# Dense layers in token blocks of 512 with a last one of 256, gated product written over the gates, weight steps a block sooner

## The chip, the cores and the metric

One core of a Trainium2 chip runs the whole kernel in one launch. The metric is device time in microseconds, from the start of the launch to its end. TensorE (PE) multiplies, VectorE (DVE), ScalarE (ACT) and GpSimd (POOL) work on elements, SyncE (SP) issues most DMAs. Each engine takes its instructions strictly in the order in which the kernel emits them, and waits on semaphores of the others.

## The reference: what is computed

Attention with a threshold, then a layer that mixes tokens and has a wide hidden layer, then a gated layer with a causal convolution. Four batches of 576 tokens, 512 channels, 2304 tokens in all:

```python
# attention: 4 batches, 8 heads, 576 tokens, 64 channels each -> x (4, 576, 512)
h = xt @ U @ V                                  # rank 32, over tokens
u = x + h.transpose(0, 2, 1)
ch = np.maximum(u @ w_ch1, 0.0) @ w_ch2         # 512 -> 2048 -> 512
x = u + ch
...
gate_pre += conv_w[k] * xp[:, k:k + S, :]       # 5 taps, causal
gate = 1.0 / (1.0 + np.exp(-gate_pre))
val = x @ w_val
return gate * val @ w_out
```

The change concerns the part from `u @ w_ch1` on.

## The kernel before

**Operands in two halves.** The dense layers multiply in a rounded float format. To keep accuracy each operand is held as a high half (rounded) and a low half (the rest), and each product is three matmuls: high x high, high x low, low x high. `passes` (line 732) does this for one output tile of 128 channels: 4 pieces of 128 input channels by three, 12 matmuls into one PSUM bank. The weights are the stationary side (128 x 128), the tokens the moving one.

**Token blocks.** Tokens lie along the free dimension. All 2304 are cut into NN blocks of NB = 384 (lines 70 and 71), six of them, whatever the batch bounds; `runs(n)` (line 709) gives the pieces of a block by batch.

**Chunks.** The hidden layer of 2048 is done in four chunks of 512 (`items`: chunk c outside, block n inside). For each (c, n), `h1` (line 740) makes the hidden block: 4 x 12 matmuls into the tiles named `a`, per tile a ReLU on ScalarE into the high half of `h` and the low half on VectorE. `ch` (line 789) multiplies it by the second weight, 4 x 12 matmuls into tiles named `c`, and VectorE adds them into `y`. `back` of an item is emitted one item later, so that TensorE does h1 of block n+1 before ch of block n. `split_block` (line 718) makes the two halves of the next block's input `us` (ScalarE, then VectorE); `us` has one buffer, so it is written after the h1 that reads the last one and before the next, while TensorE does a ch.

**The front.** The first two h1 are emitted piece by piece among the last steps of attention (`dense_front`, line 752), to fill TensorE there; `mix_t` and `mix_u` (lines 521 and 531) and the copies of lines 439, 481, 540 and 547 are attention's own.

**Weights.** They come as 64 bit floats. `weight_rows` (line 153) is a generator: a DMA, then about ten steps on ScalarE, VectorE and GpSimd (lines 99 to 127, 162, 164) that turn 128 x 512 of them into two halves. `chunk(c, part)` (line 698) puts four such generators into `work`; each `tick` advances those that live (four at most) by one step. So where weight operations stand among the others follows from where `chunk` is called and how often `tick` is. w1 and w2 have two buffers each, by turns for even and odd chunks.

**Gates.** When all of a batch's y is there (last chunk), `gate_step` (line 807) goes on with its gates, one step per call: ScalarE makes the first tap, VectorE four more (line 819), ScalarE the sigmoid. The gates are written over `u`. `tick` calls it once, or twice in proj.

**val and proj.** `val(n)` (line 852) multiplies y by w_val into tiles `v`; VectorE multiplies by the gate into one of two buffers of `ring` (line 863), ScalarE rounds that to the high half of `g`, VectorE makes the low half. `proj(n)` (line 871) multiplies by w_out, 128 tokens at a time with 512 output channels as moving columns (line 879), ScalarE copies into `ring`, and SyncE sends 256 KB out. The order at the end: val(0), the last ch, val(1), proj(0), val(2), proj(1), and so on.

Of the kernel before, what the change touches and what calls it, by code (L numbers as in the profile page):

```python
# [21 lines left out]
F32 = mybir.dt.float32  # L22
# [14 lines left out]
def attention_moe_kernel(  # L37
# [29 lines left out]
    TL = S - SM  # L67
    HS = S // 2
    T = B * S
    NB = 384  # L70
    NN = T // NB
    YP = S + KC - 1
    assert D == 64 and S == 576 and DM == 512 and R == 32 and TL == 64

# [8 lines left out]
    qscale = const.tile([128, 1], F32, name="qscale")  # L83
    cw = const.tile([128, KC, KD], F32, name="cw")
    u = const.tile([128, KD, T], F32, name="u")
    ring = const.tile([128, 2560], F32, name="ring")
    w1_0 = const.tile([128, 2, KD, FC], F32R, name="w1_0")
    w2_0 = const.tile([128, 2, KD, FC], F32R, name="w2_0")
    wst_p = ctx.enter_context(tc.tile_pool(name="wst", bufs=2))
# [60 lines left out]
        return w[0:m, 0:n]  # L150


    def weight_rows(dst, kk, src, lo_eng, *opt):
# [11 lines left out]
        done.append(0)  # L165


    class Staged:
# [524 lines left out]


    p1 = {}
    w1, w2 = [[w1_0], []], [[w2_0], []]

    def chunk(c, part):
        if c < NCH:
            src = w_ch2[c * FC:(c + 1) * FC, :] if part else w_ch1[:, 2 * c * FC:2 * (c + 1) * FC]  # L700
        else:
            src = w_out if part else w_val
        for kk in range(KD):
            work.add(weight_rows((w2 if part else w1)[c % 2], kk, src[kk * 128:(kk + 1) * 128, :],
              nc.vector if c == 0 and part else nc.gpsimd,
              *((0, 1) if c == 0 and not part else ())))


    def runs(n):
        got, done = [], 0  # L710
        while done < NB:
            b, s = divmod(n * NB + done, S)
            m = min(NB - done, S - s)
            got.append((done, m, b, s))
            done += m
        return got
# [10 lines left out]
        return t  # L727

    def u_src(n):
        return [(0, NB, u[:, :, n * NB:(n + 1) * NB])]  # L730

    def passes(ps, w, x, e):
        ops = []
        for kk in range(KD):
            wh, wl = w[:, 0, kk, e * 128:(e + 1) * 128], w[:, 1, kk, e * 128:(e + 1) * 128]
            ops += [(wh, x[:, 0, kk, :]), (wh, x[:, 1, kk, :]), (wl, x[:, 0, kk, :])]
# [3 lines left out]
    def h1(c, us):  # L740
        t = p1["h"].tile([128, 2, KD, NB], F32R, tag="h", name="h")
        for e in range(KD):
            ps = p1["a"].tile([128, 512], F32, tag="a", name="a")
            passes(ps, w1[c % 2][0], us, e)
            nc.scalar.activation(out=t[:, 0, e, :], in_=ps[:, 0:NB], func=ACTF.Relu)  # L745
            nc.vector.scalar_tensor_tensor(  # L746
                out=t[:, 1, e, :], in0=ps[:, 0:NB], scalar=0.0, in1=f(t[:, 0, e, :]), op0=ALU.max, op1=ALU.subtract
            )
            yield t


    def dense_front():
        p1["us"] = ctx.enter_context(tc.tile_pool(name="us", bufs=1, side="right"))
        p1["h"] = ctx.enter_context(tc.tile_pool(name="h", bufs=2, side="right"))
        p1["a"] = ctx.enter_context(tc.tile_pool(name="a_ps", bufs=4, space=PSUM))
        p1["t"] = []
        us = split_block(u_src(0), p1["us"])
        yield
        while len(done) < 1 + KD:
            yield  # L760
        us2 = None
        for t in h1(0, us):
# [4 lines left out]
        for t in h1(0, us2):  # L767
            yield
        p1["t"].append(t)
        yield  # L770
        p1["s"] = split_block(u_src(2), p1["us"])
# [4 lines left out]
    def dense_back():  # L776
        extra.close()
        low.close()
        big = ctx.enter_context(tc.tile_pool(name="big", bufs=1))
        p1["y"] = big.tile([128, KD, B, YP], F32, name="y")  # L780
        w1[1].append(big.tile([128, 2, KD, FC], F32R, name="w1_1"))
        w2[1].append(big.tile([128, 2, KD, FC], F32R, name="w2_1"))
        nc.gpsimd.memset(p1["y"][:, :, :, 0:KC - 1], 0.0)

    def dense():
        y = p1["y"]
        c_ps = ctx.enter_context(tc.tile_pool(name="c_ps", bufs=4, space=PSUM, side="right"))

        def ch(c, n, t):
            for e in range(KD):  # L790
                ps = c_ps.tile([128, 512], F32, tag="c", name="c")
                passes(ps, w2[c % 2][0], t, e)
# [34 lines left out]

        def tick(n=1):
            work.tick()
            for _ in range(n):  # L830
                gate_step()

# [17 lines left out]
        turn = {"g": 0, "o": 0}  # L850
# [19 lines left out]

        def proj(n, t):
            w = w2[NCH % 2][0]
            for g in range(NB // 128):
# [25 lines left out]
        work.finish()  # L899
        work.add(setup_cw())  # L900
        for idx, (c, n) in enumerate(items):
            if idx >= 2:
                for t in h1(c, us):
                    tick()
                held.append((c, n, t))
                us = split_block(u_src(items[idx + 1][1]) if idx + 1 < len(items) else y_src(0))
            if n == 1:
                chunk(c + 1, 0)
                chunk(c + 1, 1)
            if idx:  # L910
                back(*held.pop(0))
        pt = None
        for n in range(NN):
            t = val(n, us)
# [42 lines left out]
```

## Time and profile before

| | |
|---|---|
| timed runs | 880.66 us median of three, 878.94 to 881.77 |
| profiled execution | 882.26 us, its span 880.5 us |
| mean granted TensorE clock | 0.982 |
| TensorE busy | 837.9 us (95%) |
| VectorE busy | 616.9 us (70%) |
| ScalarE, GpSimd busy | 443.7 us, 212.7 us |
| bytes moved | 69.76 MB |

The page of the profile cuts the span into 40 slices of 22 us and gives each engine's busy share in tenths. In a timeline or a chain of waits each row has a start and a length in us, then the engine, the line of the kernel and how many instructions are merged; the length runs to the end of the last one. Matmuls are pipelined, so a run of them is priced by the starts of what stands before and behind, or by the chain, which gives the time until the next link. A bracket at the end names idle time ahead of the row and who ended it. Records of one engine overlap by a little under 0.1 us.

### The profile page before, as it was taken

The page shows a single profiled execution, that of the slowest core. Times are in us where ns is not written, and L with a number is a line of the kernel's source. Part 1 is how long each engine was busy: PE and PEld are TensorE (multiplying, and loading weights), DVE is VectorE, ACT ScalarE, POOL GpSimd, SP SyncE. Part 2 cuts the span into 40 slices and gives each one's busy share as a digit, 9 for nine tenths or more (in the row PEclk, how much of TensorE's full clock was granted, in tenths as well). Part 3 has the DMA queues.
Part 4 walks back from the last instruction along what each step waited for, and adds up shares of the span by engine and source line. Part 5 has one row for each costly group of instructions (what it writes and reads, how often), then busy time and mean ns, then how long its engine had stood idle before and what let it go on. Part 6 is the DMA issues. An engine that isn't in the chain of part 4 may idle for free. (4 is left out here: it accounts for less than half of the span.)

```text
span 880.5 us, 15063 instructions
## 1 busy us (share of the span) xinstructions
PE 837.9 (95%) x5480; PEld 773.9 (88%) x5480; DVE 616.9 (70%) x1368; ACT 443.7 (50%) x916; POOL 212.7 (24%) x304
## 2 busy tenths in 40 slices
PE   6868999999999999999999999999999999999998
PEld 5756878787878788889999999999999999998896
DVE  2775988989898988435664576546774489988850
ACT  2556887878888878522332333222331244435532
POOL 1323443433332322003242033202221023400000
PEclk7798999999999999999999999999999999999999
DMA  5764766675755544001121021101120012000111
GB/s 127 159 140 97 167 153 142 149 165 130 178 127 122 123 105 110 1 1 48 48 73 48 1 79 66 49 1 48 48 72 25 1 52 69 25 1 36 62 47 72
DMA packets 71076, 69.76 MB, mean 79 GB/s; under 512 B 49621, under 2 KB 54357, under 8 KB 71002
## 3 DMA queue, kind: packets, MB, share of 16 engines
q1 hardware_dynamic: 70058, 68.50, 31.8%
q8 instruction: 44, 0.72, 0.3%
q10 hardware_dynamic: 944, 0.30, 0.2%
q14 instruction: 30, 0.25, 0.1%
HBM read 35.44 MB, written 4.72 MB: 46 GB/s over the span
## 5 line engine op out<-in xcount | busy, mean ns | idle before, releaser
L738 PE MATMUL c<-h,w 128*128 128x384 f32 x1152 | 206.9, 338 | 1.2 <-ACT u L547 1.2
L738 PE MATMUL a<-us,w 128*128 128x384 f32 x1152 | 207.5, 338 | 0.0
L738 PEld LDWEIGHTS c<-h,w 128*128 128x128 f32 x1152 | 202.9, 188 | 1.5 <-ACT u L547 1.5
L738 PEld LDWEIGHTS a<-us,w 128*128 128x128 f32 x1152 | 202.7, 188 | 0.4 <-issue 0.4
L745 ACT ACTIVATE h<-a 128x384 fp32r<-128x384 f32 x96 | 47.0, 490 | 177.6 <-PE a L738 177.6
L127 POOL TENSOR_TENSOR wf<-wf,wt 128x512 f32<-128x512 f32 (+2 forms) x42 | 60.0, 1429 | 284.6 <-DVE wt L122 281.0
L403 POOL TENSOR_TENSOR th<-nm,tau_eff 128x1 f32<-128x1 f32 x144 | 74.6, 519 | 221.6 <-DVE ns L388 220.9
L413 DVE SCALAR_TENSOR_TENSOR e<-ns,th,e 128x576 f32<-128x576 f32 x144 | 121.0, 840 | 9.6 <-ACT e L402 8.6
L388 DVE TENSOR_SCALAR_CACHE_REDUCE ns<-s 128x576 f32<-128x576 f32 x144 | 107.7, 748 | 26.6 <-PE s L374 25.9
L746 DVE SCALAR_TENSOR_TENSOR h<-a,h 128x384 fp32r<-128x384 f32 x96 | 53.4, 556 | 104.1 <-ACT h L745 104.1
L402 ACT ACTIVATE e<-ns,nm 128x576 f32<-128x576 f32 x144 | 111.4, 773 | 28.5 <-DVE ns L388 26.1
L374 PE MATMUL s<-st 128*128 128x288 f32 x504 | 100.3, 321 | 2.3 <-DMA st<-qk 1.3
L430 PE MATMUL xm<-idn,e 128*128 128x128 f32 x576 | 88.3, 276 | 2.9 <-DVE qk L299 1.1
L439 ACT ACTIVATE pt<-xm 128x512 f32<-128x512 f32 x144 | 84.6, 587 | 6.3 <-PE xm L430 3.4
L374 PEld LDWEIGHTS s<-st 128*128 128x128 f32 x504 | 72.7, 192 | 15.0 <-issue 5.6
L430 PEld LDWEIGHTS xm<-idn,e 128*128 128x128 f32 x576 | 70.2, 142 | 6.4 <-ACT pt L439 2.3
L484 PE MATMUL o<-pt,vt 128*64 128x256 f32 (+1 forms) x768 | 71.6, 337 | 0.0
L484 PEld LDWEIGHTS o<-pt,vt 128*64 128x64 f32 x768 | 42.4, 141 | 25.5 <-issue 11.7
L796 DVE TENSOR_TENSOR y<-c,y 128x384 f32<-128x384 f32 (+1 forms) x96 | 40.5, 447 | 32.1 <-PE c L738 32.1
L162 ACT ACTIVATE w<-wf 128x512 fp32r<-128x512 f32 x40 | 25.2, 629 | 72.6 <-POOL wf L127 72.6
L819 DVE SCALAR_TENSOR_TENSOR u<-y,cw,u 128x576 f32<-128x576 f32 x64 | 58.5, 920 | 0.4
L723 DVE TENSOR_TENSOR us<-u,us 128x768 fp32r<-128x768 f32 x48 | 53.6, 1156 | 5.9 <-ACT us L722 5.9
(99 smaller groups left out, 1038.4 us busy)
## 6 DMA issues: line engine op xcount, KB each, us to landing
raw<-in_moe_w_ch_dram SPq DMA_DIRECT2D x32, 512.0 KB, 3.9
st<-qk SPq DMA_DIRECT2D x32, 256.0 KB, 4.1
st<-qk SPq DMA_DIRECT2D x16, 432.0 KB, 4.0
st<-qk SPq DMA_DIRECT2D x48, 144.0 KB, 4.3
st<-qk SPq DMA_DIRECT2D x16, 288.0 KB, 4.9
out_dram<-ring SPq DMA_DIRECT2D x18, 256.0 KB, 2.0
qn<-in_q_dram SPq DMA_DIRECT2D x32, 128.0 KB, 3.5
kn<-in_k_dram SPq DMA_DIRECT2D x32, 128.0 KB, 4.0
```

Source lines behind the costliest of these rows:

```text
L127: nc.gpsimd.tensor_tensor(out=dst, in0=dst, in1=tf, op=ALU.add)
L374: nc.tensor.matmul(s[:, n, 0:HS], lhs, rhs[:, n * HS:(n + 1) * HS], start=(m == 0), stop=(m == len(ops) - 1))
L388: nc.vector.tensor_scalar(out=ns.rearrange("p (a b) -> p a b", a=2), in0=s, scalar1=-1.0, scalar2=3.0e38, op0=ALU.mult, op1=ALU.min, accum ...
L402: nc.scalar.activation(out=row(p, i), in_=d["ns", i], func=ACTF.Exp, bias=nm[:, 0:1], scale=-1.0)
L403: nc.gpsimd.tensor_tensor(out=th, in0=nm, in1=tau_eff, op=ALU.add)
L413: nc.vector.scalar_tensor_tensor(out=e, in0=d.pop(("ns", i)), scalar=d.pop(("th", i))[:, 0:1], in1=e, op0=ALU.is_le, op1=ALU.mult, accum_o ...
L430: nc.tensor.transpose(x[:, j * 128:(j + 1) * 128], e[:, c + j * 128:c + (j + 1) * 128], idn)
L439: later(s + 1, 0, lambda: nc.scalar.activation(out=dst, in_=x.rearrange("p (j c) -> p j c", j=4), func=ACTF.Copy), "x")
L484: nc.tensor.matmul(o, lhs, rhs, start=False, stop=stop)
L723: nc.vector.tensor_tensor(out=t[:, 1, e:e + 2, o:o + m], in0=s[:, e:e + 2], in1=f(t[:, 0, e:e + 2, o:o + m]), op=ALU.subtract,)
L738: nc.tensor.matmul(ps[:, 0:NB], lhs, rhs, start=(m == 0), stop=(m == len(ops) - 1))
L819: nc.vector.scalar_tensor_tensor(out=g, in0=y[:, e, b, k:k + S], scalar=cw[:, k, e:e + 1], in1=g, op0=ALU.mult, op1=ALU.add)
```

## The change

NB becomes 512, so that there are four blocks of 512 tokens and a last one of 256; all operations take the block's own size. Other parts of the change:

- The gated product is written over the gates in `u`, not into `ring`, which is cut to what proj and the set-up need.
- w2's second buffer moves to a pool of its own on the other side of SBUF.
- `chunk(c + 1)` is called when n = 0, behind `back`, not when n = 1, ahead of it. Every second tick advances the weight steps twice. `need` makes sure that the steps of a weight are emitted before the matmuls that read it.
- ch calls `tick(2)`: two gate steps per tile.

```diff
-    NB = 384
-    NN = T // NB
+    NB = 512
+    NN = -(-T // NB)
+    size = [min(NB, T - n * NB) for n in range(NN)]
...
-    ring = const.tile([128, 2560], F32, name="ring")
+    ring = const.tile([128, 1280 + S // 2], F32, name="ring")
...
+    def need(c, part):
+        while len(rows[c, part]) < KD:
+            work.tick()
...
-            nc.tensor.matmul(ps[:, 0:NB], lhs, rhs, start=(m == 0), stop=(m == len(ops) - 1))
+            nc.tensor.matmul(ps[:, 0:m1], lhs, rhs, start=(m == 0), stop=(m == len(ops) - 1))
...
-        w2[1].append(big.tile([128, 2, KD, FC], F32R, name="w2_1"))
+        w2_p = ctx.enter_context(tc.tile_pool(name="w2", bufs=1, side="right"))
+        w2[1].append(w2_p.tile([128, 2, KD, FC], F32R, name="w2_1"))
...
         def ch(c, n, t):
+            need(c, 1)
...
-                tick()
+                tick(2)
...
         def tick(n=1):
             work.tick()
+            turn["w"] ^= 1
+            if turn["w"]:
+                work.tick()
...
-                passes(ps, w1[NCH % 2][0], ys, e)
-                o = 2 * DM + turn["g"] % 2 * NB
-                g = ring[:, o:o + NB]
-                turn["g"] += 1
-                nc.vector.tensor_tensor(out=g, in0=ps[:, 0:NB], in1=u[:, e, n * NB:(n + 1) * NB], op=ALU.mult)
-                nc.scalar.activation(out=t[:, 0, e, :], in_=g, func=ACTF.Copy)
-                nc.vector.tensor_tensor(out=t[:, 1, e, :], in0=g, in1=f(t[:, 0, e, :]), op=ALU.subtract)
+                m = size[n]
+                passes(ps, w1[NCH % 2][0], ys, e, m)
+                g = u[:, e, n * NB:n * NB + m]
+                nc.vector.tensor_tensor(out=g, in0=ps[:, 0:m], in1=g, op=ALU.mult)
+                nc.scalar.activation(out=t[:, 0, e, 0:m], in_=g, func=ACTF.Copy)
+                nc.vector.tensor_tensor(out=t[:, 1, e, 0:m], in0=g, in1=f(t[:, 0, e, 0:m]), op=ALU.subtract)
...
         for idx, (c, n) in enumerate(items):
+            need(c, 0)
             if idx >= 2:
-                for t in h1(c, us):
+                for t in h1(c, us, n):
                     tick()
                 held.append((c, n, t))
                 us = split_block(u_src(items[idx + 1][1]) if idx + 1 < len(items) else y_src(0))
-            if n == 1:
+            if idx:
+                back(*held.pop(0))
+            if n == 0:
                 chunk(c + 1, 0)
                 chunk(c + 1, 1)
-            if idx:
-                back(*held.pop(0))
+        need(NCH, 0)
+        need(NCH, 1)
```

What this moves on TensorE is shown by the end of the program. Before, from the last h1 (`a`) over the last two ch (`c`) to the first proj (`p`); `v` is val:

```order
L738 MATMUL a<-us,w_1_5525 128x384 x48
L738 MATMUL c<-h,w_1_5526 128x384 x48
L738 MATMUL v<-us,w_0_66 128x384 x48
L738 MATMUL c<-h,w_1_5526 128x384 x48
L738 MATMUL v<-us,w_0_66 128x384 x48
L879 MATMUL p<-w_0_67,g 128x512 x36
```

And now the same stretch:

```order
L745 MATMUL a<-us,w_1_5525 128x256 x48
L745 MATMUL c<-h,w_1_5529 128x512 x48
L745 MATMUL v<-us,w_0_66 128x512 x48
L745 MATMUL c<-h,w_1_5529 128x256 x48
L745 MATMUL v<-us,w_0_66 128x512 x48
L891 MATMUL p<-w_0_67,g 128x512 x48
```

The sequence is the same; what stands between the two val blocks is now the narrow ch.

VectorE, before, from the split for the first val block (`us<-y`) to the first val product: `u<-y,cw,u` is a gate step, `y<-c,y` the sum of ch, `wt` a weight operation.

```order
L723 TENSOR_TENSOR us<-y,us 128x768 x2
L796 TENSOR_TENSOR y<-c,y 128x192 x2
L122 SCALAR_TENSOR_TENSOR wt<-raw,wt 128x512
L819 SCALAR_TENSOR_TENSOR u<-y,cw,u 128x576
L796 TENSOR_TENSOR y<-c,y 128x192 x2
L819 SCALAR_TENSOR_TENSOR u<-y,cw,u 128x576
L796 TENSOR_TENSOR y<-c,y 128x192 x2
L819 SCALAR_TENSOR_TENSOR u<-y,cw,u 128x576
L796 TENSOR_TENSOR y<-c,y 128x192 x2
L819 SCALAR_TENSOR_TENSOR u<-y,cw,u 128x576
L863 TENSOR_TENSOR ring<-v,u 128x384
```

VectorE now, from the c block of n = 2 in the last chunk, where the last weight operations stand:

```order
L806 TENSOR_TENSOR y<-c,y 128x128
L806 TENSOR_TENSOR y<-c,y 128x384
L113 TENSOR_SCALAR wt<-wf 128x512
L109 SCALAR_TENSOR_TENSOR wf<-raw,wt 128x512
L123 SCALAR_TENSOR_TENSOR wt<-raw,wt 128x512
L113 TENSOR_SCALAR wt<-wf 128x512
L829 SCALAR_TENSOR_TENSOR u<-y,cw,u 128x576 x2
L806 TENSOR_TENSOR y<-c,y 128x128
L806 TENSOR_TENSOR y<-c,y 128x384
L123 SCALAR_TENSOR_TENSOR wt<-raw,wt 128x512
L829 SCALAR_TENSOR_TENSOR u<-y,cw,u 128x576 x2
```

The last weight operation has moved from the ch ahead of the first val block to the ch before that one, and gate steps stand two by two.

## Rows read from the trace of the kernel before

**Rows 1.** The page: TensorE's busy time, its 40 slices, the granted clock.

```profile
PE 837.9 (95%) x5480; PEld 773.9 (88%) x5480; DVE 616.9 (70%) x1368; ACT 443.7 (50%) x916; POOL 212.7 (24%) x304
...
PE   6868999999999999999999999999999999999998
...
PEclk7798999999999999999999999999999999999999
```

**Rows 2.** Waits of TensorE from 355 us on: us in total, times, longest.

```profile
PE c L738 <- ACT u L547: 1.2, 1, 1.2
PE t L525 <- DVE ring L496: 1.1, 1, 1.1
PE v L738 <- DVE us L723: 1.0, 1, 1.0
PE xk L447 <- ACT pt L439: 0.6, 1, 0.6
```

**Rows 3.** The chain that ended last, its end: start, us, what.

```profile
792.55 8.40 PE p L879 x36
800.95 8.45 PE v L738 x48
...
876.83 0.60 ACT ring L883
```

**Rows 4.** Busy time by engine, 720 to 760 us: PE, PEld, DVE, ACT, POOL.

```profile
720.00:760.00 40.00, 40.00 (x229) 40.00 (x228) 40.00 (x63) 20.38 (x34) 13.28 (x8) 1.00 0.17 53
```

**Rows 5.** Timeline of TensorE, scores (288 columns) and transpositions (128 columns).

```profile
334.76 1.04 PE L374 MATMUL s<-qk,bd 128*128 128x288 f32 x6
...
341.17 0.78 PE L374 MATMUL s<-st 128*128 128x288 f32 x4
341.79 0.60 PE L430 MATMUL xm<-idn,e 128*128 128x128 f32 x4
342.22 0.27 PE L447 MATMUL xk<-idn,e 128*128 128x128 f32 x1
```

**Rows 6.** Timeline of the front, ScalarE and VectorE.

```profile
357.27 1.58 ACT L722 ACTIVATE us<-u 128x768 fp32r<-128x768 f32 x2
...
374.26 0.56 DVE L746 SCALAR_TENSOR_TENSOR h<-a,h 128x384 fp32r<-128x384 f32 x1 [1.78 <-ACT h L745]
...
383.39 0.49 ACT L745 ACTIVATE h<-a 128x384 fp32r<-128x384 f32 x1 [2.51 <-PE a L738]
```

**Rows 7.** Timeline of VectorE around the first val block.

```profile
764.16 1.81 DVE L723 TENSOR_TENSOR us<-y,us 128x768 fp32r<-128x768 f32 x2
...
767.75 0.61 DVE L796 TENSOR_TENSOR y<-c,y 128x192 f32<-128x192 f32 x2
...
771.84 1.32 DVE L819 SCALAR_TENSOR_TENSOR u<-y,cw,u 128x576 f32<-128x576 f32 x1
773.08 0.54 DVE L863 TENSOR_TENSOR ring<-v,u 128x384 f32<-128x384 f32 x1
...
774.69 0.81 DVE L819 SCALAR_TENSOR_TENSOR u<-y,cw,u 128x576 f32<-128x576 f32 x1
775.42 0.55 DVE L863 TENSOR_TENSOR ring<-v,u 128x384 f32<-128x384 f32 x1
```

**Rows 8.** Timeline of TensorE, val and the last ch.

```profile
765.35 8.61 PE L738 MATMUL v<-us,w 128*128 128x384 f32 x48
773.79 8.62 PE L738 MATMUL c<-h,w 128*128 128x384 f32 x48
...
792.39 8.56 PE L879 MATMUL p<-w,g 128*128 128x512 f32 x36
```

**Rows 9.** Timeline of GpSimd, the last weight passes.

```profile
768.96 3.59 POOL L164 TENSOR_TENSOR w<-wf,w 128x512 fp32r<-128x512 f32 x2
```

**Rows 10.** Groups by line: the loads of weights (count, busy us, mean ns).

```profile
L738 PEld LDWEIGHTS c<-h,w 128*128 128x128 f32 x1152 | 202.9, 188 | 1.5 <-ACT u L547 1.5
L374 PEld LDWEIGHTS s<-st 128*128 128x128 f32 x504 | 72.7, 192 | 15.0 <-issue 5.6
```

More of the change, by code (lines that the diff above doesn't have):

```diff
@@ L150, in convert, with weight_rows @@
         return w[0:m, 0:n]
-    def weight_rows(dst, kk, src, lo_eng, *opt):
+    def weight_rows(got, dst, kk, src, lo_eng, *opt):
         raw = yield from wstage(FC)
@@ L165, in weight_rows @@
         done.append(0)
+        got.append(0)
     class Staged:
@@ L695, in attention_moe_kernel @@
     p1 = {}
+    rows = {}
     w1, w2 = [[w1_0], []], [[w2_0], []]
@@ L703, in chunk @@
         for kk in range(KD):
-            work.add(weight_rows((w2 if part else w1)[c % 2], kk, src[kk * 128:(kk + 1) * 128, :],
+            work.add(weight_rows(rows.setdefault((c, part), []), (w2 if part else w1)[c % 2], kk, src[kk * 128:(kk + 1) * 128, :],
               nc.vector if c == 0 and part else nc.gpsimd,
               *((0, 1) if c == 0 and not part else ())))
+    def need(c, part):
+        while len(rows[c, part]) < KD:
+            work.tick()
     def runs(n):
         got, done = [], 0
-        while done < NB:
+        while done < size[n]:
             b, s = divmod(n * NB + done, S)
-            m = min(NB - done, S - s)
+            m = min(size[n] - done, S - s)
             got.append((done, m, b, s))
@@ L729, in u_src, with passes @@
     def u_src(n):
-        return [(0, NB, u[:, :, n * NB:(n + 1) * NB])]
-    def passes(ps, w, x, e):
+        return [(0, size[n], u[:, :, n * NB:n * NB + size[n]])]
+    def passes(ps, w, x, e, m1):
         ops = []
@@ L735, in passes, with h1 @@
             wh, wl = w[:, 0, kk, e * 128:(e + 1) * 128], w[:, 1, kk, e * 128:(e + 1) * 128]
-            ops += [(wh, x[:, 0, kk, :]), (wh, x[:, 1, kk, :]), (wl, x[:, 0, kk, :])]
+            ops += [(wh, x[:, 0, kk, 0:m1]), (wh, x[:, 1, kk, 0:m1]), (wl, x[:, 0, kk, 0:m1])]
         for m, (lhs, rhs) in enumerate(ops):
-            nc.tensor.matmul(ps[:, 0:NB], lhs, rhs, start=(m == 0), stop=(m == len(ops) - 1))
-    def h1(c, us):
+            nc.tensor.matmul(ps[:, 0:m1], lhs, rhs, start=(m == 0), stop=(m == len(ops) - 1))
+    def h1(c, us, n):
+        m = size[n]
         t = p1["h"].tile([128, 2, KD, NB], F32R, tag="h", name="h")
@@ L743, in h1 @@
             ps = p1["a"].tile([128, 512], F32, tag="a", name="a")
-            passes(ps, w1[c % 2][0], us, e)
-            nc.scalar.activation(out=t[:, 0, e, :], in_=ps[:, 0:NB], func=ACTF.Relu)
+            passes(ps, w1[c % 2][0], us, e, m)
+            nc.scalar.activation(out=t[:, 0, e, 0:m], in_=ps[:, 0:m], func=ACTF.Relu)
             nc.vector.scalar_tensor_tensor(
-                out=t[:, 1, e, :], in0=ps[:, 0:NB], scalar=0.0, in1=f(t[:, 0, e, :]), op0=ALU.max, op1=ALU.subtract
+                out=t[:, 1, e, 0:m], in0=ps[:, 0:m], scalar=0.0, in1=f(t[:, 0, e, 0:m]), op0=ALU.max, op1=ALU.subtract
             )
@@ L761, in dense_front @@
         us2 = None
-        for t in h1(0, us):
+        for t in h1(0, us, 0):
             yield
@@ L766, in dense_front @@
         p1["t"].append(t)
-        for t in h1(0, us2):
+        for t in h1(0, us2, 1):
             yield
@@ L789, in ch @@
         def ch(c, n, t):
+            need(c, 1)
             for e in range(KD):
                 ps = c_ps.tile([128, 512], F32, tag="c", name="c")
-                passes(ps, w2[c % 2][0], t, e)
+                passes(ps, w2[c % 2][0], t, e, size[n])
                 for o, m, b, s in runs(n):
@@ L848, in setup_cw @@
             done.append(0)
-        turn = {"g": 0, "o": 0}
+        turn = {"o": 0, "w": 0}
         def val(n, ys):
@@ L858, in val @@
                 ps = p1["a"].tile([128, 512], F32, tag="a", name="v")
[L859 to L865 removed]
+                m = size[n]
+                passes(ps, w1[NCH % 2][0], ys, e, m)
[3 more added lines that the diff above has]
+                nc.vector.tensor_tensor(out=t[:, 1, e, 0:m], in0=g, in1=f(t[:, 0, e, 0:m]), op=ALU.subtract)
                 tick()
@@ L872, in proj @@
             w = w2[NCH % 2][0]
-            for g in range(NB // 128):
+            for g in range(size[n] // 128):
                 ps = c_ps.tile([128, 512], F32, tag="c", name="p")
```

## Prediction, written before the changed kernel ran

> **What bounds the kernel now.** I read the page first: TensorE is busy 837.9 us of the span, its slices are nines from 400 us on, and the granted clock is at its upper level, 2.4 GHz, throughout that part [rows 1]. The change touches nothing ahead of 360 us: in the built order the rows of TensorE up to the dense front read alike. So the question is what TensorE's time behind 360 us is made of. The four longest waits of TensorE from 355 us on sum to 3.9 us, one wait each [rows 2]; the chain of work shows, from 784 us to the end, matmuls back to back and then one copy of 0.60 us [rows 3]. Everything else is streaming: by the code 6 blocks x 48 x 9 = 2592 matmuls of 384 columns (L738: two layers of four chunks, and val) and 18 x 12 = 216 of 512 (L879). VectorE is full for a while (40.00 of 40.00 us, [rows 4]), but TensorE is full in the same stretch, so that costs something only where TensorE waits for it: at 784 us, for the split of the second val block (v <- DVE us, [rows 2]).
>
> **Matmuls: fewer and wider.** The chain gives the price by width. 48 matmuls of 384 columns take 8.45 us, 176.0 ns each; 36 of 512 take 8.40 us, 233.3 ns each [rows 3]. That is 57.3 ns for 128 columns, 0.448 ns a column, and 176.0 - 384 x 0.448 = 4.0 ns that a matmul costs beside its columns. The same line gives 133 ns at 288 columns; the trace has 1.04 us for six such against 0.78 us for four, 130 ns each [rows 5], so the line holds well below 384. At 256 it gives 118.7 ns.
> The columns stay the same; only the number of matmuls falls. Before: 2592 x 176.0 ns = 456.2 us. After: four of five blocks have 512 columns and one 256, so 4 x 48 x 9 = 1728 wide ones, 403.2 us, and 432 narrow ones, 51.3 us, 454.5 us in all. The gain is 1.7 us, 432 fewer matmuls at 4.0 ns. Bounds: 256 columns can't be expected under half of 512, 116.7 ns (0.9 us more gain). Upwards, the nearest row below is a transposition of 128 columns: the next row starts 0.43 us after four of them, 108 ns each [rows 5]; a straight line from there to 130 ns at 288 gives 126 ns at 256, 3.2 us lost. And the 512 columns of L738 might cost 4/3 of 176.0, 234.7 ns: 2.3 us lost. I take 118.7 and 233.3, since the rows nearest in width stand behind them.
> Here the Trainium skill speaks for much more. "TensorE: Matmul & The Clock Gate", section "Back-to-back issue gap", gives a sustained spacing of about 81 ns at 128 columns and 131 ns at 512, in which columns cost little and each instruction much; as an estimate from that page the change would save some 28 us. The same section's gap for a lone matmul, N / 2.4 + 2.5 ns, would save 432 x 2.5 ns = 1.1 us. The trace differs from the first by its 233.3 ns at 512 columns [rows 3], and the measurement decides.
>
> **VectorE and ScalarE work per block.** Two operations of 768 columns take 1.81 us on VectorE, 0.91 each, and one of 384 takes 0.54 to 0.56 us [rows 6, 7]; so 128 more columns cost about 0.12 us. ScalarE has 1.58 us for two and 0.49 us [rows 6]: about 0.10 us. With five blocks for six there are fewer of them; none of that is on the path, except at the waits below.
>
> **The front (360 to 385 us): longer waits.** Three waits of TensorE hang there on chains that grow with the block. (a) Ahead of h1, ScalarE splits block 0 in two operations (1.58 us at 357.27, [rows 6]); the copy that TensorE then waits for (L439, 0.6 us of idling, [rows 2]) stands right behind them. Two of 1024 columns take 0.4 us longer, and h1 starts 0.4 us later. (b) mix_t waits for L496 on VectorE, which is queued behind the low half of h, which waits for ScalarE's high half of the same piece [rows 6]: 0.10 + 0.12 us more. More matmuls ahead of it don't cover that, since the chain begins where they end. (c) The first c waits for L547 on ScalarE, which stands behind an h of 0.49 us [rows 2, 6]: 0.10 us more. Sum: 0.7 us lost; between nothing (if L439 has slack that the wait hides) and 1.0.
>
> **The val stage: a shorter cover, a shorter queue.** From the last c block (773.79) to the first proj (792.39) stand two blocks of 8.45 us, but the stretch takes 18.60 us [rows 8]: 1.7 us lost, 1.0 of it in the wait of the second val block for its split [rows 2]. The cause is VectorE's queue: the first val product is ready near 767.6 us (a quarter of a block after 765.35, [rows 8]), and VectorE reaches it at 773.08, 5.5 us late [rows 7]. One piece of val takes VectorE 2.34 us there (773.08 to 775.42: product, ScalarE's copy, low half, a gate step), and TensorE 8.45 / 4 = 2.11 us, so it can't catch up. Part of the lag is GpSimd: a gate step takes 0.81 us when GpSimd rests, and 1.32 us while GpSimd's weight passes from 768.96 us on run [rows 7, 9]; the weight steps of the last chunk run into the gates.
> After the change the weight steps come sooner (half as many again per tick, and added a block earlier), so that their last ones stand in the c block of n = 2. No wait of TensorE names a weight [rows 2], so sooner is worth nothing there; it counts only by what it takes from the gates. I go through VectorE's order as built. In that c block: 8 gate steps of 0.73 us (0.81 less the 0.08 by which records overlap), 4 sums into y of 0.65 in two pieces each (0.61 for two of 192 in [rows 7], 0.12 for 128 more columns, less 0.08), 5 weight operations of 512 columns (0.60 each by the same count) and some 2 us held up by four passes of GpSimd (0.5 us each, as above): 13.4 us, begun 2.8 us into a block of 11.2, so 5.0 us are left over. From there to the first val product TensorE has 5.7 + 11.2 + 2.8 = 19.7 us, VectorE 12 gate steps (8.8), 4 low halves of 256 (1.4), 2 splits of 1024 (2.1) and 4 sums (2.6): 14.9 us. It is 0.2 us late, or 2 us if GpSimd holds each step up twice as long, instead of 5.5. A piece of val then takes 2.34 + 0.34 = 2.68 us against TensorE's 2.80, so it keeps up.
> But the cover shrinks too. Between the two val blocks stands the last c block, and that is now the one of 256: 48 x 118.7 ns = 5.7 us for 8.45. From the end T of the first val block: last piece 2.7 us, split of 2 x 64 and 2 x 448 columns 2.4 us, and the lag of 0 to 2.6: ready at T + 5.1 to 7.7, its first half 1.0 us sooner, while TensorE wants the first half at T + 5.9 and the second at T + 7.1. That is a wait of 0 to 1.2 us; I take 0.7. Against 1.7 before, 1.0 us gained (0.5 to 1.7). Later val blocks have a proj of 11.2 us between them, and their VectorE work (4 x 2.68, 8 gate steps, a split of 2.2: 18.7 us) fits into 22.4.
>
> **What costs nothing.** The product of val written over the gates is the same VectorE operation with another target; nobody waits for the ring's two buffers before. The ring, the pools and `need` issue nothing. The weight DMAs on SP's queue start earlier, where TensorE never waits for them. The order of the end is unchanged: proj of the last two blocks in one run, covered, then the copy and one output.
>
> **Sum.** -1.7 - 1.0 + 0.7 = -2.0 us. On the profiled execution's 882.26 us (span 880.5 and 1.8 around it) that is 880.3; it lies 1.6 us above the median of the timed runs, 880.66, and on that scale the forecast is 878.7 us, 0.2% less. About 0.3% (2.6 us) is what a measurement of this kernel can tell from no change, so the likeliest reading is "same".
>
> **Rivals.**
> 1. All of it goes well: no wait between the val blocks (-1.7), 256 at 116.7 ns (-2.6), the front's L439 with slack (+0.3): -4.0 us, 876.7. For it: VectorE's lag by the sum above is small. Against: two bounds must be reached at once. Chance 0.25.
> 2. A floor under the 256-column matmuls, which ends on the slower side. Every matmul loads its 128 columns of weights anew, and a load is recorded at 188 ns, more than the 176.0 ns between matmuls [rows 10]; if the load is what spaces them, 432 narrow matmuls cost 176.0 instead of 118.7 ns: +24.8 us, 903.5. From 123 ns on the forecast's gain is gone, from 129 ns on the kernel is slower by 0.3%. Against: loads of the same shape are recorded at 192 ns beside 130 ns per matmul in the scores [rows 5, 10], and the transpositions follow each other in 108 ns, so the record holds waiting. Chance 0.06.
> 3. VectorE's lag stays at 5.5 us (gate steps now stand two by two, each waiting for the one before): the split is ready at T + 10.2, the wait 3.3 us instead of 1.7: -1.7 + 1.6 + 0.7 = +0.6, 881.3. Against: the sum above. Chance 0.08.
> 4. Instructions rather than columns cost: if the price rose on the line from 108 ns at 128 columns to 176.0 at 384, 0.27 ns a column, 512 would take 210 and 256 142 ns: 424.2 us, 32.0 us gained, with the other terms 848.4. The rows at 512 and 288 columns speak against it [rows 3, 5]. Chance 0.01. By the page of the Trainium skill named above it would be this way.
>
> **How the numbers follow.** The forecast has 0.60, with 877 to 881 as its own range. The range of 8 in 10 takes in rival 1, most of rival 3 and a part of the bounds of the matmul term: 876.0 to 882.2. Faster by over 0.3% means under 878.0: most of rival 1 (0.18), a fifth of the forecast (0.12), rival 4: 0.31. Slower, over 883.3: rival 2 (0.05), tails of the others (0.04): 0.09. The rest, 0.60, is within.
>
> **What would show it.** L738 in the profile after: blocks of 48 at 11.2 us and at 5.7 us; a narrow block of over 6.2 us is rival 2. The waits of TensorE: xk, t and c each a little longer, v under 1.2 us. VectorE: the first val product read within 2 us of its end, gate steps beside GpSimd few. I am wrong if a wait appears in the dense part that isn't there before (a split that misses the end of a 256 block, which covers it by 5.7 us and needs about 4), or if the wide blocks don't cost 11.2 us.

## The result, and the profile after

The changed kernel takes 869.5 us (median of four runs, 868.24 to 871.87) where the kernel before takes 880.7 us in the same session: ratio 0.9876, 95% interval 0.9863 to 0.989. That is 11.2 us less, where 2.0 us were forecast; the time lies 6.5 us below the lower end of the range, 876.0. The profiled execution has a span of 870.0 us for 880.5.

The page: TensorE's busy time and the granted clock, to be read against [rows 1].

```profile
PE 826.3 (95%) x5048; PEld 695.3 (80%) x5048; DVE 613.0 (70%) x1336; ACT 438.5 (50%) x888; POOL 212.6 (24%) x304
PEclk7797999999999999999999999999999999999999
```

TensorE is busy 11.6 us less, with the clock in nines from the fifth slice on in both. The chain that ended last says by which instructions (start, us, what), to be read against [rows 3]:

```profile
697.90 10.88 PE a L745 x48
...
789.77 10.88 PE p L891 x48
...
844.17 5.75 PE v L745 x48
```

A wide block takes 10.88 us, 226.7 ns a matmul, a narrow one 5.75 us, 119.8 ns. And proj, whose matmuls the change does not touch, takes 10.88 us for 48: **226.7 ns, where [rows 3] have 233.3 for the same instruction.** So something that the forecast held fixed has moved.

The waits of TensorE from 355 us on (total us, times, longest), against [rows 2]:

```profile
PE t L527 <- DVE ring L498: 1.3, 1, 1.3
PE c L745 <- ACT u L549: 1.3, 1, 1.3
PE v L745 <- DVE us L730: 1.1, 1, 1.1
PE xk L449 <- ACT pt L441: 1.0, 1, 1.0
PE v L745 <- ACT us L729: 0.9, 1, 0.9
```

The front's three waits grew as forecast. Ahead of the second val block there are now two waits, one for each half of the split. The timeline of TensorE there, against [rows 8]:

```profile
757.92 11.04 PE L745 MATMUL v<-us,w 128*128 128x512 f32 x48
768.80 5.91 PE L745 MATMUL c<-h,w 128*128 128x256 f32 x48
775.60 0.49 PE L745 MATMUL v<-us,w 128*128 128x512 f32 x1 [0.89 <-ACT us L729]
777.22 12.55 PE L745 MATMUL v<-us,w 128*128 128x512 f32 x47 [1.12 <-DVE us L730]
789.61 10.59 PE L891 MATMUL p<-w,g 128*128 128x512 f32 x46
```

From 768.80 to 789.61 are 20.81 us for blocks of 5.75 and 10.88: 4.2 us lost, where 1.7 were lost before. Two us are the waits. The block of 47 is long as well: the windows (PE, PEld, DVE, ACT, POOL busy; then the granted clock) show why.

```profile
768.00:780.00 12.00, 9.99 (x61) 8.76 (x60) 9.73 (x17) 5.96 (x11) 0.00 (x0) 0.89 0.00 1
780.00:790.00 10.00, 10.00 (x44) 8.22 (x43) 8.41 (x14) 3.55 (x6) 0.00 (x0) 0.96 0.00 1
```

The granted clock falls to the lower level, 1.2 GHz, for 3.4 us after the two waits. Inside the block of 47 one matmul is then followed after 529 ns and the next seven after 426 or 427 ns, where 227 is the rule: 1.7 us more. Before, one wait of 1.0 us stood there and the clock did not fall. The fall need not be in every run of the changed kernel: the four timed ones take 871.87, 870.58, 868.41 and 868.24 us with a mean granted clock of 0.980, 0.982, 0.988 and 0.988, and the profiled one is the first. Why TensorE waits, VectorE's timeline tells, against [rows 7]:

```profile
764.56 0.68 DVE L875 TENSOR_TENSOR u<-v,u 128x512 f32<-128x512 f32 x1
...
767.34 0.68 DVE L875 TENSOR_TENSOR u<-v,u 128x512 f32<-128x512 f32 x1
...
775.68 2.49 DVE L730 TENSOR_TENSOR us<-y,us 128x128 fp32r<-128x128 f32 x4
```

The first val product is ready near 760.7 (a quarter of a block after 757.92) and read at 764.56, 3.9 us late. A piece takes VectorE 2.78 us (764.56 to 767.34) and TensorE 2.72, so the lag stays, and the split starts 6.9 us after the block's end.

### The profile page after: what moved, and what is told of

The parts are those of the page before. It is cut to its first block, busy times and chain, and to the rows that moved or that the text cites. A ratio compares the mean times of both kernels' runs of the same rounds, so it can differ in the third digit from the quotient of the medians.

```text
span 870.0 us, 14167 instructions
## 1 busy us (share of the span) xinstructions
PE 826.3 (95%) x5048; PEld 695.3 (80%) x5048; DVE 613.0 (70%) x1336; ACT 438.5 (50%) x888; POOL 212.6 (24%) x304
## 4 chain that ended last, share of the span: by engine, by line
PE 74%; DVE 10%; ACT 6%; DMA 3%; SPq 3%; issue 2%; POOL 0%; ACTq 0%; DVEq 0%; POOLq 0%
PE a L745 22%; PE c L745 20%; PE o L486 6%; PE s L376 6%; PE p L891 6%; PE v L745 5%; PE xm L432 4%; DVE u L829 3%; PE o L475 2%; DVE e L415 2%; DMA raw<-in_moe_w_ch_dram 2%; DVE ns L390 2%; ACT e L404 1%; PE t L527 1%; ACT qk L291 1%
## 5 line engine op out<-in xcount | busy, mean ns | idle before, releaser
L745 PE MATMUL c<-h,w 128*128 128x512 f32 (+1 forms) x960 | 200.9, 368 | 1.3 <-ACT u L549 1.3
L745 PE MATMUL a<-us,w 128*128 128x512 f32 (+1 forms) x960 | 201.5, 369 | 0.0
L745 PEld LDWEIGHTS c<-h,w 128*128 128x128 f32 x960 | 167.4, 189 | 31.6 <-ACT u L549 1.7
L745 PEld LDWEIGHTS a<-us,w 128*128 128x128 f32 x960 | 167.2, 189 | 30.2 <-issue 0.4
L753 ACT ACTIVATE h<-a 128x512 fp32r<-128x512 f32 (+1 forms) x80 | 44.2, 554 | 195.2 <-PE a L745 195.2
L754 DVE SCALAR_TENSOR_TENSOR h<-a,h 128x512 fp32r<-128x512 f32 (+1 forms) x80 | 50.9, 636 | 106.8 <-ACT h L753 106.8
L128 POOL TENSOR_TENSOR wf<-wf,wt 128x512 f32<-128x512 f32 (+2 forms) x42 | 56.1, 1336 | 257.2 <-DVE wt L123 257.2
L376 PEld LDWEIGHTS s<-st 128*128 128x128 f32 x504 | 72.5, 193 | 15.3 <-issue 5.9
L165 POOL TENSOR_TENSOR w<-wf,w 128x512 fp32r<-128x512 f32 x36 | 54.0, 1513 | 10.0 <-ACT w L163 10.0
L806 DVE TENSOR_TENSOR y<-c,y 128x64 f32<-128x64 f32 (+4 forms) x96 | 39.8, 448 | 21.3 <-PE c L745 21.3
L745 PE MATMUL v<-us,w 128*128 128x512 f32 (+1 forms) x240 | 52.1, 377 | 2.0 <-DVE us L730 1.1
```

The costliest lines, as they stand in the source:

```text
L128: nc.gpsimd.tensor_tensor(out=dst, in0=dst, in1=tf, op=ALU.add)
L376: nc.tensor.matmul(s[:, n, 0:HS], lhs, rhs[:, n * HS:(n + 1) * HS], start=(m == 0), stop=(m == len(ops) - 1))
L745: nc.tensor.matmul(ps[:, 0:m1], lhs, rhs, start=(m == 0), stop=(m == len(ops) - 1))
```

## Where the time went, term by term

| us | forecast | by the traces |
|---|---|---|
| matmuls of the dense part and proj | -1.7 | -14.2 |
| front waits | +0.7 | +0.7 |
| val stage | -1.0 | +2.5 |
| sum | -2.0 | -11.0 (spans: -10.5) |

Of the +2.5 us of the val stage, 1.7 are the lower clock's, in this one execution.

The first term is 2592 x 176.0 + 216 x 233.3 ns = 506.6 us before, and 36 x 10.88 + 9 x 5.75 + 216 x 0.2267 = 492.4 us after. The starts of successive matmuls show what lies inside the means (ns from one start to the next):

```
before, 384 columns:  173 174 175 182 176 | 173 174 175 182 176 | 173 ...
before, proj, 512:    229 238 | 229 238 | 229 237 | 229 238 ...
after, 512 columns:   226 227 226 227 227 227 226 227 227 ...
after, 256 columns:   119 120 119 121 119 121 120 120 119 ...
```

After, the matmuls of a width are alike but for the first few behind a narrow block, and three widths lie on one line: 119.8 at 256, 226.7 at 512, which is 0.4176 ns a column and 12.9 ns a matmul, and 160.4 + 12.9 = 173.3 at 384, the smallest step of before. Before, some matmuls of each group of five (384) or two (512) cost more: by these starts 13 ns in five, and 13 ns in two.

**Theory "place".** The diff has a side effect that neither the order nor the waits show. `ring` stands ahead of the weights in SBUF, and goes from 2560 to 1568 columns: 3968 bytes per partition, 15.5 times 256. As built, the first byte of all weight tiles stood at 96 modulo 256 before, that of the token tiles (`us`, `h`, `g`, from the other side) at 224; now w1 and w2 stand at 224 too (w2's second buffer by its own move). If that is the cause, shifting the weights by 128 bytes alone gives the gain, and shifting them back takes it away. **Rival "width":** the new widths, the order or the clock free TensorE of something.

## Experiments

Ratios are to the kernel before in the same session (880.6 to 881.0 us), with 95% intervals; runs 6 and 7 were timed once and have none.

**1. The kernel before, weights 128 bytes lower.**

```diff
-    ring = const.tile([128, 2560], F32, name="ring")
+    ring = const.tile([128, 2528], F32, name="ring")
```

> The kernel before with `ring` 32 columns (128 bytes) shorter and nothing else, so that the weights, and all that stands behind the ring in SBUF, lie 128 bytes lower: 224 instead of 96 bytes past a multiple of 256, as the token tiles do and as in the changed kernel. Theory 'place' (the unchanged proj matmuls became cheaper, 226.7 for 233.3 ns, because weights and token tiles stand alike modulo 256 bytes): 48 matmuls of 384 columns take 8.32 us instead of 8.45, 36 of 512 take 8.16 instead of 8.40, and the whole 2592 x 2.67 + 216 x 6.67 ns = 8.4 us less, about 872.3. Theory 'width' (wide blocks or their row pitch make the matmuls cheaper): nothing changes, 880.7 and 8.45.

874.5 us, ratio 0.9922 (0.9907 to 0.9937). The end of its chain:

```profile
844.59 8.34 PE v L738 x48
852.93 16.38 PE p L879 x72
```

The blocks of 384 go from 8.45 to 8.34 us (8.32 within the chunks, 173.3 ns), proj from 233.3 to 227.5 ns (16.38 us for 72): 7.0 + 1.2 us less streaming, with not one instruction changed. It does not all arrive: the val stage loses 4.2 us here, not 1.7. VectorE's queue there is as long as it was and TensorE comes sooner, so it waits 1.8 us in all, not 1.0; and behind the waits the granted clock falls for 3.4 us, as in the changed kernel, which makes the block of 47 1.7 us longer.

**2. The changed kernel, weights 128 bytes higher**, so at 96 again; w2's second buffer, on the other side, stays at 224.

```diff
-    ring = const.tile([128, 1280 + S // 2], F32, name="ring")
+    ring = const.tile([128, 1312 + S // 2], F32, name="ring")
```

> The changed kernel with `ring` 32 columns (128 bytes) longer and nothing else: the weights lie at 96 bytes past a multiple of 256 again, but for w2's second buffer, which has a pool of its own on the other side and stays at 224. 'Place': wide blocks of 11.2 us instead of 10.88 in all h1, val and proj and in the ch of even chunks, 10.88 still in the ch of odd chunks (1 and 3); 28 blocks x 48 x 6.67 ns + 216 x 6.67 ns = 10.4 us more, about 880. 'Width': 10.88 us throughout, 869.5.

878.6 us, ratio 0.9967 (0.9951 to 0.9983): eight to nine of the eleven us are gone, where 'place' expected 10.4. Most of its dearer wide blocks take 11.14 to 11.16 us, not 11.2. The chain has its own control, since in odd chunks `c` reads the buffer that did not move:

```profile
681.61 11.14 PE a L745 x48
692.75 10.89 PE c L745 x48
...
796.27 11.16 PE p L891 x48
```

**3. The changed kernel with blocks of 384.**

```diff
-    NB = 512
+    NB = 384
```

> The changed kernel with NB = 384, all other parts of the change kept (gated product over the gates, weight steps sooner, two gate steps per tile of ch, shorter ring, so weights at 224 past a multiple of 256). 'Place': blocks of 8.32 us, proj 8.16 for 36; 8.4 us less than before from the place, and what the other parts do to the val stage on top (1.7 us of loss there before): 870 to 874. 'Width': blocks of 8.45, 880 to 882. By 'place' the rest of the gain, 869.5 against this, is what the block size itself gives: 432 matmuls fewer at 13.3 ns, 5.8 us, less what the front and the val stage lose by it.

877.3 us, ratio 0.9958 (0.9943 to 0.9973). The blocks have the prices of 'place' (8.34 and 8.20 us), but the time lies outside the ranges of both theories, and above that of run 1, which has the same blocks and prices. VectorE is late ahead of the last h1, a place where it was not before; on the chain there stand weight steps and gate pairs, which come denser in time with shorter blocks, but no run takes the two apart:

```profile
744.59 0.44 PE L745 MATMUL a<-us,w 128*128 128x384 f32 x1 [1.91 <-ACT us L729]
746.20 9.70 PE L745 MATMUL a<-us,w 128*128 128x384 f32 x47 [1.17 <-DVE us L730]
```

The granted clock falls here too, for 3.4 us, and the block of 47 takes 9.5 us instead of 8.1.

**4 and 5. Which place counts.** The kernel before with the token tiles 128 bytes lower, the weights untouched (run 4), and with both lower (run 5, with run 1's `ring`):

```diff
+        ctx.enter_context(tc.tile_pool(name="pad", bufs=1, side="right")).tile([128, 32], F32, name="pad")
```

> The kernel before with 128 unused bytes ahead of the token tiles (us, h, g), which move from 224 to 96 past a multiple of 256, while the weights stay at 96. 'Place' in the form that the two must stand alike: as fast as with the shorter ring, 8.32 us a block, about 872.3. 'Place' in the form that only the weights' own place counts: 8.45, 880.7. 'Width': 8.45, 880.7.

> The kernel before with both moves of the two earlier runs at once: the weights 128 bytes lower and the token tiles 128 bytes lower as well, so that both have changed their place and stand towards each other as in the kernel before. Theory 'difference' (what counts is whether weights and tokens start alike modulo 256 bytes): the gain of either move alone is gone, blocks of 48 matmuls of 384 columns take 8.45 us (176 ns each), 36 of 512 take 8.40 us, time 880 to 882 us. Rival 'own place' (the old places 96 of the weights and 224 of the tokens are bad in themselves): 8.32 and 8.20 us, time 873 to 876 us.

Run 4: 875.2 us, ratio 0.9925 (0.9911 to 0.994). Run 5: 880.75 us, ratio 1.0003 (0.9994 to 1.0012). Chain rows of run 4, then of run 5:

```profile
844.49 8.34 PE v L738 x48
852.83 16.38 PE p L880 x72
```

```profile
850.07 8.45 PE v L738 x48
858.51 16.82 PE p L880 x72
```

Either move alone gives the gain, both together give nothing: it is the distance of the two operands that counts, not where either stands. That it counts modulo 256 bytes and not 512 shows in the changed kernel: as built, w1's second buffer stands 256 bytes from the tokens modulo 512, and its blocks take 10.88 us like the others (`a` at 697.90).

**6 and 7. Other distances**, timed once each: the changed kernel with small pads. Run 6 has w1 of even chunks at +32 from the tokens, w2 of even chunks (and w_out) at +64, w1 of odd chunks at +96, w2 of odd chunks at 0; run 7 has +160, +192, +224 and 0.

```diff
-    ring = const.tile([128, 1280 + S // 2], F32, name="ring")
+    ring = const.tile([128, 1288 + S // 2], F32, name="ring")
     w1_0 = const.tile([128, 2, KD, FC], F32R, name="w1_0")
+    const.tile([128, 8], F32, name="pad0")
...
+        big.tile([128, 8], F32, name="pad1")
         p1["y"] = big.tile([128, KD, B, YP], F32, name="y")
...
+        w2_p.tile([128, 16], F32, name="pad2")
```

(In run 7 the first is 1320. The last pad leaves w2's second buffer at distance 0, as built.)

> The changed kernel with small pads, so that the first byte of the weights stands at other distances from that of the tokens modulo 256: w1 of even chunks (and w_val) +32 bytes, w2 of even chunks (and w_out) +64, w1 of odd chunks +96, w2 of odd chunks 0 as it was. One run shows four distances in the lengths of blocks of 48 matmuls of 512 columns. Theory 'all or nothing' (only tiles that start alike are free): 11.2 us (233 ns) for the three that differ, 10.88 us (226.7 ns) for w2 of odd chunks; time about 877 us. Rival 'halves' (two halves of 128 bytes, a distance under 128 is free): 10.88 us everywhere, time 868 to 871 us. Rival 'graded': the extra time grows with the distance, 10.96, 11.04 and 11.12 us.

> The changed kernel with pads again, for three more distances of the weights' first byte from the tokens' modulo 256: w1 of even chunks (and w_val) +160, w2 of even chunks (and w_out) +192, w1 of odd chunks +224, w2 of odd chunks 0. At +32, +64 and +96 blocks of 48 matmuls of 512 columns took 11.20 to 11.24 us, at 0 10.88, and proj, in which w_out is the moving side, 10.99 at +64. Theory 'all or nothing': 11.2 us for the three that differ, 10.88 for w2 of odd chunks, and about 877 us. Rival 'nearness' (distance counted the shorter way round, so that +224 is as near as 32 and +192 as 64, and less is paid far from 128): +224 and +192 come out below +160, between 10.9 and 11.2. For proj at +192: 11.0 us if it goes by the shorter way round, 11.2 if the direction counts.

876.7 and 877.75 us. Chain rows of run 6 (chunk 2, then chunk 3, then proj):

```profile
590.36 11.20 PE c L746 x48
601.56 11.20 PE a L746 x48
...
674.47 5.45 PE c L746 x48
679.92 11.24 PE a L746 x48
691.16 10.91 PE c L746 x48
...
793.38 10.99 PE p L894 x48
```

And of run 7, the same places:

```profile
578.74 11.20 PE a L746 x48
589.95 11.01 PE c L746 x48
...
678.93 11.19 PE a L746 x48
690.12 10.89 PE c L746 x48
...
793.72 11.20 PE p L894 x48
```

At 512 columns only 0 is free. Counted as stationary minus moving operand, the distances 32, 64, 96, 128, 160 and 224 cost 5.4 to 7.5 ns a matmul (11.14 to 11.24 us, with run 2 for 128) and 192 costs 2.3 to 2.7 (10.99 and 11.01). Proj has the sides exchanged, tokens stationary and w_out moving: there the weights' +64 is 192 and costs 10.99 us, their +192 is 64 and costs 11.20. So the direction counts; that 192 alone is cheaper neither theory had. At 256 columns it is the other way: narrow blocks at distance 0 take 5.74 or 5.75 us in all these runs, at the other distances 5.45 to 5.77, so up to 6.3 ns a matmul less. Nor is it the distance alone there, since the narrow `c` at +64 takes 5.65 us in chunk 0 of run 6 and 5.45 in chunk 2.

**8. The changed kernel with the weight steps as before.**

```diff
-            turn["w"] ^= 1
-            if turn["w"]:
-                work.tick()
...
+            if n == 1:
+                chunk(c + 1, 0)
+                chunk(c + 1, 1)
             if idx:
                 back(*held.pop(0))
-            if n == 0:
-                chunk(c + 1, 0)
-                chunk(c + 1, 1)
```

> The changed kernel with the weight steps as they were before: the weights of the next chunk are called at n = 1 ahead of the ch, and each tick advances them once. Nine weight operations then stand on VectorE between the last gate step and the first val product. Theory 'VectorE late': the first val product is read some 5 us later than in the changed kernel (8 to 9 us behind its end instead of 3.9), and the waits ahead of the second val block grow by as much: 874 to 877 us. Rival 'weights don't matter' (no wait names a weight, TensorE's own price makes the whole gain): 868 to 871 us. So the run shows what the earlier weight steps are worth within the change.

892.9 us, ratio 1.0144 (1.0127 to 1.0161): far beyond either. Its two new waits:

```profile
PE v L745 <- ACT us L729: 14.6, 1, 14.6
PE c L745 <- ACT w L163: 4.6, 1, 4.6
```

The weights of chunk 1 now miss their first ch (the wait on `w`). And VectorE is 15.3 us behind at the first val product, which is ready near 766.7 and read at 781.98; in the changed kernel it is 3.9. It does not pause on the way. The nine late weight operations behind the last gate step take 5.2 us, which is what the theory had counted; the rest comes from weight operations further ahead and from gate steps stretched beside GpSimd's passes (pairs of 2.58 and 2.95 us).

```profile
781.98 0.68 DVE L872 TENSOR_TENSOR u<-v,u 128x512 f32<-128x512 f32 x1
```

The clock adds to the waits: its granted share is 0.57 from 493 to 501 us and 0.50 from 784 to 801. With five blocks for six there are fewer ticks per chunk, so "a block sooner" is what the wide blocks need: 23 us more without it.

**9. The changed kernel, no gate steps in the first val block.**

```diff
-                tick()
+                tick(n > 0)
```

> The changed kernel, but the first val block issues no gate steps (its four go into the steps behind it, where later blocks ask for them). Theory 'VectorE late' (the second val block waits for its split because VectorE reads the first val product 3.9 us late and a piece of 2.78 us with a gate step can't catch up with TensorE's 2.72): a piece takes about 2.0 us, the last one ends near T + 4.5 instead of T + 6.9, the two waits of 0.9 and 1.1 us go, and so does the fall of the granted clock behind them: 3 to 4 us off in the profiled execution, 2 to 3.5 off the median, 866 to 867.5 us. Rival 'gates return' (the four gate steps are only moved, and the third val block or its gates then come late): the same 868 to 870 us, with a new wait behind the second val block.

867.1 us, ratio 0.9846 (0.9831 to 0.9861), the fastest of all. A piece takes 2.06 us, and the split keeps ahead of TensorE:

```profile
763.62 0.68 DVE L875 TENSOR_TENSOR u<-v,u 128x512 f32<-128x512 f32 x1
...
765.68 0.68 DVE L875 TENSOR_TENSOR u<-v,u 128x512 f32<-128x512 f32 x1
...
772.47 2.10 DVE L730 TENSOR_TENSOR us<-y,us 128x896 fp32r<-128x896 f32 x2 [0.15 <-ACT us L729]
```

```profile
767.86 5.92 PE L745 MATMUL c<-h,w 128*128 128x256 f32 x48
773.61 11.06 PE L745 MATMUL v<-us,w 128*128 128x512 f32 x48
```

No wait is left between the val blocks or behind them, and the clock does not fall. The profiled span is 5.1 us shorter, the median 2.4; the fall of the clock is in the profiled execution of the changed kernel, and need not be in its others.

**10. The changed kernel, one gate step per tile in ch.**

```diff
-                tick(2)
+                tick()
```

> The changed kernel with one part undone: ch issues one gate step per tile, not two. Eight gate steps fewer then stand on VectorE ahead of the first val product, some 6.5 us of its time at 0.8 us each. Theory 'VectorE late': the first val product is read as soon as it is there (0 to 0.5 us behind its end, not 3.9), the waits ahead of the second val block go, 866.5 to 868 us, like the run without gates in val 0. Rival 'gates needed early': the gates of the second batch, now asked for inside the second val block, hold up its products, and a wait appears ahead of the third val block or of a proj: 869 to 873 us.

868.6 us, ratio 0.9863 (0.9849 to 0.9877). VectorE now waits for the first val product, and so reads it at once:

```profile
759.57 0.69 DVE L875 TENSOR_TENSOR u<-v,u 128x512 f32<-128x512 f32 x1 [1.24 <-PE v L745]
```

```profile
795.87 10.95 PE L745 MATMUL v<-us,w 128*128 128x512 f32 x47 [0.40 <-DVE us L730]
...
818.26 0.51 PE L745 MATMUL v<-us,w 128*128 128x512 f32 x1 [0.57 <-ACT us L729]
819.27 10.96 PE L745 MATMUL v<-us,w 128*128 128x512 f32 x47 [0.51 <-DVE us L730]
```

The wait ahead of the second val block is gone, so the lag was eight gate steps long; but these are asked for later, and 1.5 us of waits stand ahead of the third and fourth blocks. Both theories hold in part.

**11. Run 1 without gate steps in the first val block:** blocks of 384, place and val stall both out of the way; run 9's edit on top of run 1's.

> Blocks of 384 throughout: the kernel before with the weights 128 bytes lower (as in the first run) and, besides, no gate steps in the first val block (as in the run that did so with the changed kernel). Theory 'width pays 13.3 ns a matmul': with place and val stall out of the way on both sides, what is left against the changed kernel without gates in val 0 (867.1 us) is the width: 432 fewer matmuls at 13.3 ns, 5.8 us, less 0.8 us of longer front waits, so 871 to 873 us here. By the sum of the first run (874.5 us, 4.2 us of it lost between the val blocks) it is 870.3 us when nothing of the stall is left. Rival 'width pays nothing' (the price per matmul is 4.0 ns as predicted, 1.7 us): 868 to 869 us.

873.2 us, ratio 0.9917 (0.9902 to 0.9931). Against run 9 that is 6.1 us. The widths give 432 x 12.9 ns = 5.6 us, the front takes 0.7 of it back, and this run still has two small val waits:

```profile
758.11 8.44 PE L738 MATMUL v<-us,w 128*128 128x384 f32 x47 [0.16 <-DVE us L723]
...
792.29 8.41 PE L738 MATMUL v<-us,w 128*128 128x384 f32 x47 [0.55 <-DVE us L723]
```

At those two the blocks of 48 take 8.78 and 9.25 us (757.61 to 766.39, 791.30 to 800.55) for 8.32: 1.4 us. The sum is 6.3 us. The price of a matmul is shown, and 4.0 ns is out.

## Why the prediction was wrong, point by point

**Matmuls: this step failed.** It drew a line through 176.0 and 233.3 ns and read 4.0 ns a matmul off it. Both prices held a surcharge from the distance of weights and tokens, 2.7 ns at 384 columns and 6.6 ns at 512, and it grew with the width in the mean, so it passed for a price of columns. Of the -14.2 us, the place gives 7.0 + 1.2 = 8.2 (run 1's prices), the fewer matmuls 5.6, and 0.4 is rounding and proj's last ns. The bounds could not hold it either: they let a wide block cost more or as much, but took proj's price as a constant of the chip, when it was one of this layout. The prediction's own sign of being wrong came: the wide blocks don't cost 11.2 us. There was a sign in the trace of before. 0.448 ns a column is more than the 0.4176 that the changed kernel shows at the same granted 2.4 GHz (one clock period is 0.417 ns), and the starts one by one are not alike. A mean from a chain hides that; a row of starts would have shown that matmuls of one width are not alike, and that the cheapest has 173 ns.

**The sentence "The ring, the pools and `need` issue nothing"** was true and beside the point: the ring's size decided the place of everything behind it. By itself that place is worth 5.8 to 6.5 us to the kernel before (runs 4 and 1), 8.2 in streaming alone, and 8 to 9 to the changed kernel (run 2), and it has nothing to do with blocks of 512.

**Front: right.** xk, t and c each a little longer, 0.7 us in all, as summed.

**Val stage: mechanism right, size and sign wrong.** The forecast had VectorE 0.2 to 2 us late; it was 3.9. VectorE's timeline from the c block of n = 2 on, which starts at 730.4:

```profile
733.48 1.29 DVE L730 TENSOR_TENSOR us<-u,us 128x512 fp32r<-128x512 f32 x2
...
737.22 2.57 DVE L829 SCALAR_TENSOR_TENSOR u<-y,cw,u 128x576 f32<-128x576 f32 x2
...
744.15 2.96 DVE L829 SCALAR_TENSOR_TENSOR u<-y,cw,u 128x576 f32<-128x576 f32 x2
...
747.69 1.66 DVE L829 SCALAR_TENSOR_TENSOR u<-y,cw,u 128x576 f32<-128x576 f32 x2
```

The sum began its count 2.8 us into that block and left out the split for the narrow one (1.29 us), which stands first: VectorE begins 4.3 us in, at 734.7, so 1.5 us later than summed. GpSimd's last passes held up three gate pairs (the middle one, at 740.98, took 2.58) by 3.1 us against the 1.66 of a pair alone, where 2 were summed. A gate step is nearer 0.77 us than 0.73, 0.8 us over 20 of them. And TensorE's faster blocks leave 0.7 us less (10.9 + 19.35 for 11.2 + 19.7). 1.5 + 1.1 + 0.8 + 0.7 on top of the forecast's 0.2 make 4.3; the five weight operations give 0.5 back, since two of them take 0.33 us and not 0.60. What is left, 3.8, is the 3.9 seen. In the val block itself the forecast's 2.68 us a piece against 2.80 became 2.78 against 2.72, so nothing was caught up. Then the waits cost more than their length, by the fall of the clock in the profiled execution. Runs 9 and 10 show the lag as the cause: without the gate steps, in either place, the wait is gone.

**Weight steps "worth nothing there": wrong as a part of this change.** In the kernel before no wait names a weight, but no run there has the weight steps alone. With five blocks a chunk they carry 23 us (run 8); with six they may cost (run 3 is 2.7 us slower than run 1, but has other parts of the change too).

**Rivals.** The val stage came out near rival 3 (lag 3.9 of its 5.5 us, waits 2.0 of its 3.3). The floor under narrow matmuls did not show: 119.8 ns, near the forecast's 118.7, while the loads of `a` and `c` are still recorded at 189 ns. That the forecast came so near was luck: its line has 8.9 ns too little a matmul and 0.030 ns too much a column, and at 256 columns the two nearly cancel. Rival 4 was right in its direction, since an instruction costs more than 4.0 ns, but 12.9 and 0.4176 a column leave columns the larger part by far. The Trainium skill, "TensorE: Matmul & The Clock Gate", section "Back-to-back issue gap", has 131 ns for sustained matmuls of 512 columns, and the trace does not agree (226.7); its gap for a lone matmul, N / 2.4 + 2.5 ns, has the slope of these runs, and a constant 10.4 ns under theirs.

**Open.** What in the chip makes the distance cost was not shown; nor why 192 is cheaper, nor whether distances below 32 bytes cost. Why the clock fell after 2.0 us of waits is not settled: in run 4 waits of 1.7 us in the same place left it at the upper level, and waits of 0.7 and 1.1 us there left it up in run 6 and were followed by a fall in run 7. How much of the 11.2 us the fall takes away in the median is open.

## What to carry to other kernels

Before a price per instruction is fitted from two means, look at the starts one by one: where they are not alike, something other than the width can be in the mean. When a tile changes size, look where the tiles behind it now start; here 128 bytes on a scratch tile were worth 6 us of 880 to the kernel before and 8 to 9 to the changed one, with no instruction changed. And when the bottleneck gets faster, count the slack of the engine behind it again, for that is where part of the gain goes.

## What the runs showed of the hardware that was not expected

- Matmuls of this form (128 x 128 weights, rounded floats) take 0.4176 ns a column and 12.9 ns each when weights and tokens start alike modulo 256 bytes, and 5.4 to 7.5 ns more each at 512 columns when they do not (2.3 to 2.7 at a distance of 192, stationary minus moving).
- At 384 columns and a distance of 128 the surcharge is 13 ns in every five matmuls, so 2.7 ns each; at 256 columns none was seen, and blocks at other distances were rather cheaper than at 0 (5.45 to 5.77 us in runs 2, 6 and 7, for 5.74 or 5.75).
- After two waits of 0.9 and 1.1 us the granted clock fell to 1.2 GHz for 3.4 us; in run 8, where a wait of 14.6 us ends at 795.4, the mean granted share over the 20 us from 780 was 0.60. With much the same waits as in the changed kernel it did not fall in runs 4 and 6.
